# A fused attention and two-expert-layer kernel: one route's search by counting on TensorE, a zero-padded key chunk, and some squares on GpSimd

## The chip, the cores and the metric

One Trainium2 chip, one core. The time is device microseconds from the first to the last instruction of one execution and what lies around it; lower is better. The kernel before has a median of 1275.76 us over 3 runs.

## What is computed

Three layers in a row, all in float32. First linear attention over 8 batches, 8 heads, 576 tokens and a head width of 64, normalized per head; then a mixture of 8 experts to which the 4608 tokens are assigned greedily, each expert taking at most 576 tokens; then a dense layer that takes the maximum of three products.

```python
def _attn_ref(q, k, v, g_norm):
    kv = np.einsum('bhsd,bhse->bhde', k, v)
    out = np.einsum('bhsd,bhde->bhse', q, kv)
    rms = np.sqrt(np.mean(out * out, axis=-1, keepdims=True) + 1e-06)
    return (out / rms * g_norm)

# mixture of experts: logits = x @ w_gate, sorted over all (token, expert) pairs
    for idx in order:
        tok, e = (int(idx) // E, int(idx) % E)
        if assigned[tok] >= 0 or counts[e] >= cap:
            continue
        assigned[tok] = e
        counts[e] += 1
    for e in range(E):
        mask = assigned == e
        out[mask] = np.maximum(x[mask] @ w1[e], 0.0) @ w2[e]

# last layer
    h = np.maximum(np.maximum(x @ w1, x @ w2), x @ w3)
    return h @ w_out
```

## The kernel before, in words

**Attention (lines 85 to 497).** Batches go in pairs (`bp`, four of them); the two batches of a pair are 1152 tokens, nine chunks of 128, and chunk 4 holds the end of one batch and the start of the next. `load` puts keys, values and queries in SBUF on the SP queue, each in a first part (`a`, five chunks) and a second part (`b`, four). `kv` (line 179) multiplies keys with values on TensorE, chunk by chunk, into one PSUM tile per batch; of chunk 4 each batch takes its own 64 rows (line 189), so one of its five matmuls has 64 rows. Every float32 matmul is two instructions. `o_tile` (line 214) multiplies one chunk of queries with the result; ScalarE squares the output (line 230) and copies it to `y` (line 234), VectorE sums the squares per head (line 235). `norm_a` and `norm_b` make the norms and the gate logits `L` per three chunks, and `y_store` writes `y` to DRAM on SP. The next pair's second query part goes into the same buffer as this pair's, and its load stands in SP's order behind this pair's stores.

**Routes.** In phase `p` the kernel picks the next expert that fills up, and the 576 tokens it takes. For that it needs the threshold logit above which a column has more than its places. Route 0 (`top_search`) runs between the attention and the experts, with nothing beside it: seven rounds, each comparing every token's key with 15 to 63 thresholds (VectorE), counting per expert with 36 matmuls whose weights are the one-hot choice (8 columns), comparing the counts with the capacity, and broadcasting the verdict with one more matmul. The routes 1 to 6 run beside the experts, in pieces: `phase` is a generator, and `tick` (line 914) runs it to its next `yield`; a tick comes after every column group of 12 big matmuls (after 24 in the output layer, none). There `search` (line 504) makes 16 steps on transposed keys: per step two sign sums on ScalarE (line 512) and one comparison on VectorE (line 514), `ce` (line 518), one matmul (line 523), and four small VectorE operations (lines 527 to 534) that give the next three thresholds. With `slow` (route 1 only) a step lasts three ticks for the first eight, otherwise two.

**Experts.** In stage `p` (0 to 7) TensorE multiplies the gathered rows `X` with `w1` (8 column blocks), the result with `w2` (4), that with the three matrices of the last layer (`W3`, 6 blocks of three), and last with `w_out`. All products are split in a high and a low part, three matmuls each (`mm3`, lines 888 to 890). VectorE rounds `H` (line 979) and `X` (line 997), and in stage 0 also splits the expert weights (line 838), which GpSimd does later.

**Decoding, in stage 0 only.** The 24 weight tiles of the last layer come as 64-bit words. A background generator (`decoder`) works on one piece per tick from the fifth on: shift (line 372, VectorE), merge (line 379, VectorE), add (line 380, GpSimd), round (lines 386 and 388, ScalarE), residual (line 394, VectorE, the first four on GpSimd; line 397, GpSimd). Its tiles share the buffer `xg` with the rows that are gathered, so `gather` may run only when all 24 are `ready`.

**Order of the work.** The order of each engine is the order of the Python calls (a manual schedule). At the end of a route `tick` calls `gather` if all 24 tiles are ready; otherwise it is called after the stage's last tick (line 1025). Then GpSimd scales the five row tiles (line 868), and the output matmuls (lines 1044 to 1046) alternate with the transposes of the next expert's rows (line 877).

## Time and profile before

| what | value |
|---|---|
| median of 3 runs | 1275.76 us (1274.73 to 1277.25) |
| the profiled execution's own time | 1274.72 us |
| its span | 1272.9 us |
| TensorE matmuls busy | 1208.8 us, 95% of the span |
| VectorE busy | 646.0 us, 51% |
| ScalarE busy | 482.3 us, 38% |
| GpSimd busy | 398.2 us, 31% |
| mean granted TensorE clock | 0.976 of full speed |

A page of the profile names each group of instructions by its line, engine and operation, and by its tiles as output<-inputs. A bracket at the end of a row of the timeline is the time its engine stood idle just before, and what it waited for. The rows of waits name the waiting instruction, then what released it, with the total, the number of times and the longest. Matmuls are pipelined, so a row's duration is longer than its distance to the next one; where a price per matmul is needed, starts are compared. TensorE is busy nearly all the time from 400 us on; before that it has gaps.

### The profile page before, as it was taken

The page shows a single profiled execution, that of the slowest core. Times are in us where ns is not written, and L with a number is a line of the kernel's source. Part 1 is how long each engine was busy: PE and PEld are TensorE (multiplying, and loading weights), DVE is VectorE, ACT ScalarE, POOL GpSimd, SP SyncE. Part 2 cuts the span into 40 slices and gives each one's busy share as a digit, 9 for nine tenths or more (in the row PEclk, how much of TensorE's full clock was granted, in tenths as well). Part 3 has the DMA queues.
Part 4 walks back from the last instruction along what each step waited for, and adds up shares of the span by engine and source line. Part 5 has one row for each costly group of instructions (what it writes and reads, how often), then busy time and mean ns, then how long its engine had stood idle before and what let it go on. Part 6 is the DMA issues. An engine that isn't in the chain of part 4 may idle for free.

```text
span 1272.9 us, 23272 instructions
## 1 busy us (share of the span) xinstructions
PE 1208.8 (95%) x8878; PEld 1136.6 (89%) x8880; DVE 646.0 (51%) x2075; ACT 482.3 (38%) x1166; POOL 398.2 (31%) x483
## 2 busy tenths in 40 slices
PE   9996698778999999999999999999999999999996
PEld 7885398777999989998999899999999899989995
DVE  2656688873576346653666167725763421121110
ACT  3547254651453136413542155314631331133110
POOL 0000123544521354135412451245214451253121
PEclk9998798889999999999999999999999999999998
DMA  9999410343330223121311232113312252023101
GB/s 342 396 380 355 150 59 25 118 148 105 109 100 26 80 75 109 34 94 54 102 65 59 64 117 84 59 47 108 100 35 70 76 161 86 1 75 109 59 1 42
DMA packets 52033, 136.15 MB, mean 107 GB/s; under 512 B 5840, under 2 KB 10448, under 8 KB 50384
## 3 DMA queue, kind: packets, MB, share of 16 engines
q1 hardware_dynamic: 44672, 110.25, 25.8%
q0 software_dynamic: 6944, 24.38, 5.7%
q8 instruction: 70, 1.15, 0.4%
q14 instruction: 43, 0.35, 0.1%
q10 hardware_dynamic: 304, 0.02, 0.0%
HBM read 111.43 MB, written 23.20 MB: 106 GB/s over the span
## 4 chain that ended last, share of the span: by engine, by line
PE 77%; DVE 12%; ACT 5%; issue 2%; DMA 2%; POOL 1%; POOLq 0%; SPq 0%; ACTq 0%; DVEq 0%
PE mm L888 19%; PE mm L890 18%; PE mm L889 18%; PE mm L1044 4%; PE mm L1046 4%; PE mm L1045 4%; PE kv L189 4%; ACT W L512 3%; PE o L225 2%; DVE T L534 2%; PE tp L877 1%; DVE w L394 1%; DVE w L379 1%; DVE dv L372 1%; DMA vtb<-vx_dram 1%
## 5 line engine op out<-in xcount | busy, mean ns | idle before, releaser
L888 PE MATMUL mm<-X,w 128*128 128x288 f32 x1152 | 346.9, 301 | 0.0
L890 PE MATMUL mm<-X,w 128*128 128x288 f32 x1152 | 341.3, 296 | 0.0
L889 PE MATMUL mm<-X,w 128*128 128x288 f32 x1152 | 341.2, 296 | 0.0
L888 PEld LDWEIGHTS mm<-X,w 128*128 128x128 f32 x1152 | 218.7, 190 | 0.4
L889 PEld LDWEIGHTS mm<-X,w 128*128 128x128 f32 x1152 | 218.2, 189 | 0.0
L890 PEld LDWEIGHTS mm<-X,w 128*128 128x128 f32 x1152 | 218.0, 189 | 0.0
L838 POOL TENSOR_TENSOR ring<-raw,ring 128x512 fp32r<-128x512 f32 x112 | 144.2, 1289 | 206.8 <-ACT ring L829 195.8
L1021 POOL TENSOR_TENSOR H<-t,H 128x288 fp32r<-128x288 f32 x96 | 77.8, 810 | 417.1 <-ACT H L1020 417.0
L1019 DVE TENSOR_TENSOR t<-mm,t 128x288 f32<-128x288 f32 x192 | 87.1, 454 | 159.5 <-PE mm L890 157.8
L888 PE MATMUL mm<-H,ring 128*128 128x288 f32 x512 | 156.5, 306 | 0.0
L888 PE MATMUL mm<-X,ring 128*128 128x288 f32 (+1 forms) x512 | 153.7, 300 | 1.6 <-ACT X L883 1.6
L889 PE MATMUL mm<-H,ring 128*128 128x288 f32 x512 | 152.3, 297 | 0.0
L890 PE MATMUL mm<-H,ring 128*128 128x288 f32 x512 | 152.1, 297 | 0.0
L890 PE MATMUL mm<-X,ring 128*128 128x288 f32 (+1 forms) x512 | 151.1, 295 | 0.6 <-DVE X L884 0.6
L889 PE MATMUL mm<-X,ring 128*128 128x288 f32 (+1 forms) x512 | 150.7, 294 | 0.0
L512 ACT ACTIVATE W<-KT,T 96x384 bf16<-96x384 f32 x168 | 102.1, 608 | 117.3 <-DVE T L534 117.3
L1020 ACT CAST H<-t 128x288 fp32r<-128x288 f32 x96 | 41.4, 432 | 231.6 <-DVE t L1019 231.6
L888 PEld LDWEIGHTS mm<-X,ring 128*128 128x128 f32 x512 | 96.4, 188 | 2.2 <-ACT X L883 2.1
L888 PEld LDWEIGHTS mm<-H,ring 128*128 128x128 f32 x512 | 98.0, 191 | 0.0
L889 PEld LDWEIGHTS mm<-H,ring 128*128 128x128 f32 x512 | 97.5, 190 | 0.0
L890 PEld LDWEIGHTS mm<-H,ring 128*128 128x128 f32 x512 | 97.2, 190 | 0.0
L890 PEld LDWEIGHTS mm<-X,ring 128*128 128x128 f32 x512 | 96.1, 188 | 1.1 <-DVE X L884 1.1
(257 smaller groups left out, 2037.4 us busy)
## 6 DMA issues: line engine op xcount, KB each, us to landing
raw<-w_dram SPq DMA_DIRECT2D x128, 256.0 KB, 2.7
ring<-wod SPq DMA_DIRECT2D x48, 512.0 KB, 3.5
xd<-y SPq DMA_DIRECT2D x36, 288.0 KB, 9.4
w<-w_dram SPq DMA_DIRECT2D x18, 512.0 KB, 8.2
qta<-qx_dram SPq DMA_DIRECT2D x4, 1280.0 KB, 15.0
qtb<-qx_dram SPq DMA_DIRECT2D x4, 1024.0 KB, 12.4
kta<-kx_dram SPq DMA_DIRECT2D x3, 1280.0 KB, 17.6
vta<-vx_dram SPq DMA_DIRECT2D x3, 1280.0 KB, 16.6
```

The source lines that it names most:

```text
L189: nc.tensor.matmul(KV[b][:, hp, :], KT[bp, o][p0:p1, c - o * CA, h], VT[bp, o][p0:p1, c - o * CA, h], start=(i == 0), stop=(i == len(cs) - 1))
L512: nc.scalar.activation(gs[:, j], KT, AF.Sign, bias=T[0:96, 1 + j:2 + j], scale=-1.0, accum_out=cnt[:, j:j + 1])
L838: (nc.gpsimd if stream[m][0] else nc.vector).tensor_sub(t[:, 1], raw, t[:, 0])
L888: nc.tensor.matmul(ps, wt[:, 0, ws], x[:, 0, xs], start=first, stop=False)
L889: nc.tensor.matmul(ps, wt[:, 1, ws], x[:, 0, xs], start=False, stop=False)
L890: nc.tensor.matmul(ps, wt[:, 0, ws], x[:, 1, xs], start=False, stop=last)
L1019: nc.vector.tensor_tensor(t2, ps[:, :HS], (t1, t1, t2)[j], op=OP.max)
L1020: nc.scalar.copy(m[:, 0, cs], t2)
L1021: nc.gpsimd.tensor_sub(m[:, 1, cs], t2, m[:, 0, cs])
L1044: nc.tensor.matmul(pss[c], l[:, 0, ls], w[:, 0, :], start=(fc == 0), stop=False)
L1045: nc.tensor.matmul(pss[c], l[:, 0, ls], w[:, 1, :], start=False, stop=False)
L1046: nc.tensor.matmul(pss[c], l[:, 1, ls], w[:, 0, :], start=False, stop=(fc == 5))
```

## The change

1. *Key chunk 4.* The first part of the keys is loaded without it (four chunks). It goes into a tile of its own, `ZK`, twice: once with the lower 64 rows and zeros above, once the other way. The zeros are set once on GpSimd; the rows come in two small transfers per pair (on ScalarE's queue for the first pair, on SP's after that). All `kv` matmuls then have 128 rows.
2. *Squares.* For the middle chunk of each three (not among the last three of all) the square is computed on GpSimd from the copied `y`. Its reduction on VectorE is put off until the next chunk's.
3. *Route 1* (`p == 1`) no longer transposes its keys; `count_search` makes seven rounds in the manner of route 0, with the route's own limits per expert. A round lasts four ticks: two from the comparison to the 36 matmuls, two from these to the broadcast. Its tables `TH`, `SV` and `th0` move to a pool that lives on, the thresholds in bfloat16. The other routes go through `sign_search`, which is the old code moved.
4. *Gather.* `tick` calls `gather` in any tick from which on the route is done and all 24 tiles are ready, and from the seventh tick after that scales one row tile per tick; what is left is scaled at the end of the stage.

```diff
+    ZK = []
+    for i in range(2):
+        z = ld.tile([128, 2, DM], F32, name="zk%d" % i)
+        nc.gpsimd.memset(z[64:128, 0], 0.0)
+        nc.gpsimd.memset(z[0:64, 1], 0.0)
+        ZK.append(z)
...
-                nc.sync.dma_start(KT[bp, 0][:, :, h0:h1], kx[bp, :, 0:CA, h0:h1])
+                nc.sync.dma_start(KT[bp, 0][:, :, h0:h1], kx[bp, :, 0:CA - 1, h0:h1])
                 nc.sync.dma_start(VT[bp, 0][:, :, h0:h1], vx[bp, :, 0:CA, h0:h1])
+            for r in range(2):
+                p = slice(64 * r, 64 * r + 64)
+                (nc.sync if bp else nc.scalar).dma_start(ZK[bp % 2][p, r], kx[bp, p, CA - 1])
...
-            for i, (c, p0, p1) in enumerate(cs):
+            for i, c in enumerate(cs):
                 o = int(c >= CA)
-                nc.tensor.matmul(KV[b][:, hp, :], KT[bp, o][p0:p1, c - o * CA, h], VT[bp, o][p0:p1, c - o * CA, h],
+                kt = ZK[bp % 2][:, r, h] if c == CA - 1 else KT[bp, o][:, c - o * CA, h]
+                nc.tensor.matmul(KV[b][:, hp, :], kt, VT[bp, o][:, c - o * CA, h],
...
-        nc.scalar.activation(sq, pv[:, :, :, 0:128], AF.Square)
+        pool = gi == 1 and c < NT - 3
+        if not pool:
+            nc.scalar.activation(sq, pv[:, :, :, 0:128], AF.Square)
...
-        nc.vector.tensor_reduce(SS[0][:, gi], sq.rearrange("p a b (h d) -> p (a b h) d", d=D),
-                                axis=AX, op=OP.add)
+        if pool:
+            ys = Y[0][:, gi, :, 0:128].rearrange("p (a b) d -> p a b d", a=2)
+            nc.gpsimd.tensor_mul(sq, ys, ys)
+        RQ.append((SS[0][:, gi], sq))
+        while RQ and not pool:
+            ss, sq = RQ.pop(0)
+            nc.vector.tensor_reduce(ss, sq.rearrange("p a b (h d) -> p (a b h) d", d=D), axis=AX, op=OP.add)
...
+    def count_search(g2, K, L2, oh):
...
+        for i in range(7):
+            J = STEPS[i - 1][1] if i else J0
...
+                if ns is None:
+                    nc.vector.tensor_tensor(gs[-1], kc, th, op=OP.is_ge)
+                else:
+                    nc.vector.scalar_tensor_tensor(gs[-1], kc, ns, th, op0=OP.subtract, op1=OP.is_ge)
+                if not i:
+                    yield
+            if ns is not None:
+                nc.vector.tensor_scalar(K, K, ns, None, op0=OP.subtract)
+            yield
+            yield
+            pc = rps.tile([128, 512], F32, name="rps")
+            for c in range(NT):
+                nc.tensor.matmul(pc[0:E, 0:J], oh[:, :, c], gs[c // nt][:, c % nt, :], start=(c == 0),
+                                 stop=(c == NT - 1))
+            ex = rt.tile([E, 64], BF, name="ex8")
+            nc.vector.tensor_scalar(ex[:, 0:J], pc[0:E, 0:J], lim, None, op0=OP.is_gt)
+            yield
+            yield
+            pb = rps.tile([128, 512], F32, name="rps")
+            nc.tensor.matmul(pb[:, 0:J], ones8, ex[:, 0:J], start=True, stop=True)
...
+            nc.vector.scalar_tensor_tensor(sc[:, 0:J], pb[:, 0:J], 0.5, SV[:, i:i + 1].to_broadcast([128, J]),
+                                           op0=OP.is_ge, op1=OP.mult, accum_out=ns)
...
+            if p == 1:
+                for r in count_search(g2, sf, best, oh):
...
+            else:
+                flags = yield from sign_search(g2, V, sf, best, oh, REM2)
...
             except StopIteration:
                 route = None
-                if len(ready) == 24:
-                    gather(len(XG) // 5)
+        if route is None and 0 < len(IDX) < E + 1 and len(XG) < 5 * len(IDX) and len(ready) == 24:
+            fetch[:] = [[len(IDX) - 1, 0, list(range(5))]]
+            gather(len(IDX) - 1)
```

Three places show what the engines get in another order.

VectorE in stage 0, one search step of route 1 before: from the comparison that follows a new threshold (line 514, tile `W`) to the next threshold (line 534, `T`). `ce` feeds the search matmul; line 394 is a weight residual, line 372 a decode shift, line 379 a decode merge.

```order
L514 TENSOR_SCALAR W_2806,cnt<-KT,T_2803 96x384
L1019 TENSOR_TENSOR t_2720<-mm,t_2720 128x288
L379 SCALAR_TENSOR_TENSOR w_22_1224<-w_22_1224,dv 128x512
L518 TENSOR_TENSOR ce<-BM,cnt 96x24
L394 TENSOR_TENSOR w_11_2848<-dv,w_11_2848 128x512
L372 TENSOR_SCALAR dv<-w_23_1226 128x512
L527 TENSOR_TENSOR ex<-rps,REM_1925 128x24
L529 TENSOR_REDUCE an<-ex 128x3
L531 TENSOR_SCALAR ex,tot<-an 128x3
L534 TENSOR_SCALAR T_2863<-SC,T_2803,tot 128x4
```

The same engine now, one round in the W3 layer: verdict (line 654), comparison (635), shift of the keys (639); then, past other work (rounding of X, 1086; merges, 397; shifts, 390; maxima, 1108; residual, 412), the comparison of the counts (647).

```order
L654 SCALAR_TENSOR_TENSOR scr,ns<-rps,SV 128x15
L635 SCALAR_TENSOR_TENSOR W_2821<-K_2699,ns,TH 128x540
L639 TENSOR_SCALAR K_2699<-K_2699,ns 128x36
L1086 TENSOR_TENSOR X<-mm,X 128x288
L397 SCALAR_TENSOR_TENSOR w_20_1232<-w_20_1232,dv 128x512
L390 TENSOR_SCALAR dv<-w_11_1234 128x512
L647 TENSOR_SCALAR ex_2901<-rps,lim_2035 8x15
L1108 TENSOR_TENSOR t_2827<-mm,t_2826 128x288
L397 SCALAR_TENSOR_TENSOR w_11_1234<-w_11_1234,dv 128x512
L1108 TENSOR_TENSOR t_2827<-mm,t_2827 128x288
L412 TENSOR_TENSOR w_10_2938<-dv,w_10_2938 128x512
L390 TENSOR_SCALAR dv<-w_21_1236 128x512
```

The five small operations and `ce` of a step are gone from between the decode rows; a round has one comparison and three small operations, and two ticks' work of others stands between the comparison and the verdict on the counts.

SP, from the loads for the third pair to its predecessor's second query part (`qtb`); `DMAHW` numbers are the eight completion lanes, and an entry waits for the transfer that used its lane last. Before:

```order
L98 DMA kta<-kx_dram 128x2560
L99 DMA vta<-vx_dram 128x2560 [waits DMAHW3_49]
L271 DMA xd<-y 128x576 [waits DMAHW4_49,Pool_49]
L271 DMA xd<-y 128x576 [waits DMAHW5_49,Activation_49]
L271 DMA xd<-y 128x576 [waits DMAHW6_49,Activation_49]
L271 DMA xd<-y 128x576 [waits DMAHW7_49,Pool_49]
L271 DMA xd<-y 128x576 [waits DMAHW0_49,Activation_49]
L271 DMA xd<-y 128x576 [waits DMAHW1_49,Activation_49]
L107 DMA qtb<-qx_dram 128x4x512 [waits DMAHW2_49,PE_49]
```

Now:

```order
L104 DMA kta<-kx_dram 128x2048 [waits DMAHW6_49]
L105 DMA vta<-vx_dram 128x2560 [waits DMAHW7_49]
L108 DMA zk_132<-kx_dram 64x512 [waits DMAHW0_49]
L108 DMA zk_132<-kx_dram 64x512 [waits DMAHW1_49]
L289 DMA xd<-y 128x576 [waits DMAHW2_49,Activation_49,Pool_49]
L289 DMA xd<-y 128x576 [waits DMAHW3_49,Activation_49]
L289 DMA xd<-y 128x576 [waits DMAHW4_49,Activation_49]
L289 DMA xd<-y 128x576 [waits DMAHW5_49,Activation_49,Pool_49]
L289 DMA xd<-y 128x576 [waits DMAHW6_49,Activation_49]
L289 DMA xd<-y 128x576 [waits DMAHW7_49,Activation_49]
L116 DMA qtb<-qx_dram 128x4x512 [waits DMAHW0_49,PE_49]
```

The two `zk` transfers stand behind the values, and `qtb` waits for the lane of the first of them, where it waited for the lane of the keys (`kta`).

GpSimd at the end of stage 0: subtractions for H (line 1021, now 1110), the gather (862, now 945) and the scaling of the gathered rows (868, now 951). Before:

```order
L1021 TENSOR_TENSOR H<-t_3388,H 128x288
L1023 CAST LO<-H 128x2x64
L1021 TENSOR_TENSOR H<-t_3467,H 128x288
L1021 TENSOR_TENSOR H<-t_3515,H 128x288
L1023 CAST LO<-H 128x2x64
L862 DMA xg<-xd,idx 128x576 x5
L868 TENSOR_TENSOR xg<-xg 128x4x128 x5
L838 TENSOR_TENSOR ring<-raw,ring 128x512 x4
```

Now:

```order
L398 TENSOR_TENSOR dv<-w_17_3336 128x512
L1110 TENSOR_TENSOR H<-t_3359,H 128x288
L945 DMA xg<-xd,idx 128x576 x5
L1110 TENSOR_TENSOR H<-t_3420,H 128x288
L1112 CAST LO<-H 128x2x64
L1110 TENSOR_TENSOR H<-t_3489,H 128x288
L1110 TENSOR_TENSOR H<-t_3535,H 128x288
L1112 CAST LO<-H 128x2x64
L951 TENSOR_TENSOR xg<-xg 128x4x128 x3
L1110 TENSOR_TENSOR H<-t_3585,H 128x288
L951 TENSOR_TENSOR xg<-xg 128x4x128 x2
L1110 TENSOR_TENSOR H<-t_3634,H 128x288
L1112 CAST LO<-H 128x2x64
```

The gather moved ahead of the last five H subtractions, and the scalings between them.

## Rows read from the trace of the kernel before

**Rows 1.** Timeline of TensorE (start us, us, engine, line, what): where stages begin

```profile
157.56 0.39 PE L888 MATMUL mm<-X,ring 128*128 128x256 f32 x1 [0.78 <-ACT X L883]
...
164.44 0.29 PE L888 MATMUL mm<-X,ring 128*128 128x288 f32 x1
...
327.24 0.38 PE L888 MATMUL mm<-X,ring 128*128 128x288 f32 x1
...
464.89 0.38 PE L888 MATMUL mm<-X,ring 128*128 128x288 f32 x1
...
597.17 0.38 PE L888 MATMUL mm<-X,ring 128*128 128x288 f32 x1
```

**Rows 2.** Waits of TensorE, 150 to 335 us: total us, times, longest

```profile
PE rps L523 <- DVE ce L518: 18.7, 9, 5.5
PE tp L877 <- POOL xg L868: 4.0, 1, 4.0
```

**Rows 3.** Timeline of TensorE at two search steps of stage 0

```profile
185.76 0.19 PE L523 MATMUL rps<-ce,ones 96*128 96x24 bf16 x1
...
186.02 0.29 PE L889 MATMUL mm<-X,ring 128*128 128x288 f32 x1
186.15 0.29 PE L890 MATMUL mm<-X,ring 128*128 128x288 f32 x1
...
238.05 0.20 PE L523 MATMUL rps<-ce,ones 96*128 96x24 bf16 x1 [5.48 <-DVE ce L518]
```

**Rows 4.** Busy us by window: PE, PEld, DVE, ACT, POOL, clock, DMA share, GB/s

```profile
200.00:210.00 10.00, 7.32 (x39) 7.09 (x38) 8.43 (x25) 4.43 (x12) 2.08 (x2) 0.71 0.08 26
...
30.00:60.00 30.00, 27.64 (x214) 24.70 (x213) 17.39 (x53) 17.41 (x38) 0.82 (x4) 1.00 1.02 395
```

**Rows 5.** Timeline of TensorE in the attention

```profile
16.33 0.49 PE L189 MATMUL kv<-vta,kta 64*128 64x128 f32 x2
16.74 1.16 PE L189 MATMUL kv<-vtb,ktb 128*128 128x128 f32 x8
17.74 0.60 PE L200 MATMUL bt<-ident,BD 128*128 128x128 f32 x4
...
55.68 1.22 PE L225 MATMUL o<-BD,qtb 128*128 128x144 f32 x8 [0.79 <-DMA qtb<-qx_dram]
...
80.97 1.22 PE L225 MATMUL o<-BD,qtb 128*128 128x144 f32 x8 [0.33 <-DMA qtb<-qx_dram]
82.11 0.45 PE L341 MATMUL rps<-G,oh 128*8 128x63 bf16 x9
```

**Rows 6.** Waits, all engines, 0 to 150 us

```profile
PE o L225 <- ACT y L234: 2.0, 4, 1.3
```

**Rows 7.** Chain that ended last, in order of time: one burst of 36 small matmuls

```profile
422.96 1.00 PE rps L656 x36
```

**Rows 8.** VectorE's groups, 157 to 304 us (busy us, mean ns, idle before)

```profile
L379 DVE SCALAR_TENSOR_TENSOR w<-w,dv 128x512 int32<-128x512 int32 x24 | 20.3, 847 | 0.0
L394 DVE TENSOR_TENSOR w<-dv,w 128x512 fp32r<-128x512 f32 x14 | 14.1, 1004 | 9.2 <-ACT w L386 9.1
...
L372 DVE TENSOR_SCALAR dv<-w 128x512 int32<-128x512 int32 x19 | 10.3, 541 | 0.0
L838 DVE TENSOR_TENSOR ring<-raw,ring 128x512 fp32r<-128x512 f32 x13 | 9.5, 736 | 0.0
...
L979 DVE SCALAR_TENSOR_TENSOR H<-mm,H 128x288 fp32r<-128x288 f32 (+2 forms) x16 | 7.2, 454 | 2.6 <-ACT H L976 2.3
```

**Rows 9.** Timeline of VectorE in route 0: the comparison in three pieces

```profile
119.71 1.78 DVE L583 SCALAR_TENSOR_TENSOR W<-H,ns,TH 128x372 bf16<-128x372 f32 x3
```

**Rows 10.** GpSimd's groups, 155 to 330 us: scaling of the gathered rows

```profile
L868 POOL TENSOR_TENSOR xg<-xg 128x512 f32<-128x512 f32 x5 | 5.1, 1050 | 0.0
```

**Rows 11.** Waits of the SP queue, 0 to 150 us

```profile
SPq L107 <- DMA kta<-kx_dram: 5.4, 2, 2.7
```

More of the change, by code (lines that the diff above doesn't have):

```diff
@@ L502, in bc, with search @@
         return ap[:, :, None].to_broadcast([128, E, NT])
-    def search(KT, i0, i1, REM2, slow):
+    def search(KT, i0, i1, REM2):
         T = SC[:, i0]
@@ L677, in finish, with sign_search @@
         yield
+    def sign_search(g2, V, sf, best, oh, REM2):
+        KT = []
+        for i, key in enumerate((sf, best)):
+            K = V.rearrange("p e c -> p (e c)").rearrange("p (g e c) -> p g e c", g=3, e=E)
+            for g in range(3):
+                gs = slice(12 * g, 12 * g + 12)
+                nc.vector.tensor_mul(K[:, g], oh[:, :, gs], key[:, None, gs].to_broadcast([128, E, 12]))
+            yield
+            yield
+            pt = rps.tile([128, 512], F32, name="rps")
+            for g in range(3):
+                nc.tensor.transpose(pt[0:96, g * 128:g * 128 + 128], K[:, g].rearrange("p e c -> p (e c)"),
+                                    ident)
+            KT.append(rt.tile([128, 384], F32, name="KT", tag="KT" + str(i))[0:96])
+            nc.scalar.copy(KT[i], pt[0:96, 0:384])
+            yield
+        b1 = None
+        for r in search(KT[0], 0, 11, REM2):
+            if r is None:
+                yield
+            else:
+                b1 = r
+        H1 = rt.tile([128, 1], F32, name="H1")
+        nc.vector.tensor_scalar(H1, b1, 0.5, None, op0=OP.max)
+        nc.vector.scalar_tensor_tensor(KT[1], KT[0], H1[0:96], KT[1], op0=OP.is_equal, op1=OP.mult)
+        yield
+        nc.vector.tensor_scalar(KT[0], KT[0], H1[0:96], 3000.0, op0=OP.is_gt, op1=OP.mult)
+        nc.vector.tensor_add(KT[0], KT[0], KT[1])
+        t = rt.tile([128, NT], F32, name="kt")
+        nc.vector.scalar_tensor_tensor(t, sf, H1, best, op0=OP.is_equal, op1=OP.mult)
+        nc.vector.tensor_scalar(sf, sf, H1, 3000.0, op0=OP.is_gt, op1=OP.mult)
+        nc.vector.tensor_add(sf, sf, t)
+        yield
+        b2 = None
+        for r in search(KT[0], 11, 16, REM2):
+            if r is None:
+                yield
+            else:
+                b2 = r
+        L1 = rt.tile([128, 1], F32, name="L1")
+        nc.vector.tensor_scalar(L1, b2, 1.0, None, op0=OP.add)
+        return commit(g2, sf, L1, oh)
     def phase(p):
@@ L712, in phase @@
             yield
-            KT = []
-            for i, key in enumerate((sf, best)):
-                K = V.rearrange("p e c -> p (e c)").rearrange("p (g e c) -> p g e c", g=3, e=E)
-                for g in range(3):
-                    gs = slice(12 * g, 12 * g + 12)
-                    nc.vector.tensor_mul(K[:, g], oh[:, :, gs], key[:, None, gs].to_broadcast([128, E, 12]))
-                yield
-                yield
-                pt = rps.tile([128, 512], F32, name="rps")
-                for g in range(3):
-                    nc.tensor.transpose(pt[0:96, g * 128:g * 128 + 128], K[:, g].rearrange("p e c -> p (e c)"),
-                                        ident)
-                KT.append(rt.tile([128, 384], F32, name="KT", tag="KT" + str(i))[0:96])
-                nc.scalar.copy(KT[i], pt[0:96, 0:384])
-                yield
@@ L912, in body @@
     beat = 0
+    fetch = []
     def tick():
@@ L918, in tick @@
             bg_piece(1)
+        for f in fetch:
+            f[1] += 1
+            if f[1] > 6 and f[2]:
+                scale(f[0], f[2].pop(0))
         if route is not None:
@@ L1024, in body @@
         drain()
-        if (p + 1, 0) not in XG and p + 1 < E:
-            gather(p + 1)
         if p + 1 < E:
-            for c in range(5):
-                scale(p + 1, c)
+            if (p + 1, 0) not in XG:
+                gather(p + 1)
+                fetch[:] = [[p + 1, 0, list(range(5))]]
+            while fetch[0][2]:
+                scale(p + 1, fetch[0][2].pop(0))
         odd = p % 2
```

78 lines of the change are left out of this document (42 added, 36 removed).

## The prediction

> **What bounds the kernel now.** I read the starts of the stages first, then who waits for whom on TensorE, then single places on its timeline. A stage is one expert; it begins with the first big matmul of the first layer. Stage 0 begins at 157.56 us, stage 1 at 327.24, stage 2 at 464.89, stage 3 at 597.17 [rows 1]. Stage 2 does the work of stage 0 (four output tiles, one search beside it) in 132.28 us; stage 0 takes 169.68 us. These 37.4 us are what the search part of the change can reach. In the waits of TensorE over stage 0, 18.7 us in 9 waits stand at the matmul of a search step that needs `ce` from VectorE, and 4.0 us at the transposes of the next expert's rows, which wait for GpSimd [rows 2]; the longest single wait is 5.48 us [rows 3]. The waits also cost clock: between 200 and 210 us TensorE was busy 7.32 of 10 us and the granted clock was 0.71 of full, a mix of its levels 1.2 and 2.4 GHz [rows 4]. So the excess is 18.7 + 4.0 booked, some 4 at the start (below), and the rest, about 11 us, lower clock and short gaps.
>
> The attention ahead of it has two limits that lie close together. TensorE stops at the second part of the queries of two batch pairs until it has landed, 0.79 us at 55.68 and 0.33 us at 80.97, while the DMA engines are booked full (share 1.02, 395 GB/s from 30 to 60 us) [rows 4, 5]. ScalarE holds TensorE up for 2.0 us in 4 waits [rows 6].
>
> **The change part by part.** All sums are against the profiled execution, 1274.7 us (span 1272.9); the median of the runs shown is 1.0 above it.
>
> *Search of the second route.* Sixteen steps of counting by signs become seven rounds of 36 small matmuls and one broadcast matmul. Added on TensorE: the first round has 63 columns, and nine such matmuls show 0.45 us [rows 5], so 36 cost 1.8; the other six have 31 or 15 columns, and a burst of 36 with 36 columns takes 1.00 us in the chain [rows 7], so 6.0. A lone small matmul between big ones: from the search matmul at 185.76 to the second big one after it at 186.02 are 0.26 us where big ones follow each other in 0.13 [rows 3], so it costs 0.13; seven broadcasts cost 0.9. Together 8.7 us. Removed: 16 search matmuls at 0.13, 2.1 us (six transposes go too; not counted).
>
> The waits. A step today passes three queues (VectorE sets the threshold, ScalarE makes two sign sums, VectorE makes `ce`) within 36 or 24 big matmuls. A round passes VectorE twice (compare; then the verdict), and 24 big matmuls, 24 x 0.13 = 3.1 us, stand before each of its two stops on TensorE: 14 stops. Whether VectorE keeps up is a count of its rows. A round lasts 48 x 0.13 + 1.1 = 7.4 us on TensorE. In the w2 layer VectorE has in it two decode merges (0.847 each), two residual subtractions of decoded weights (1.004), two decode shifts (0.541), two splits of expert weights (0.736) and two roundings of X (0.45, as those of H) [rows 8], 7.2 us, and of the search the compare and four small operations. The compare of 540 elements is three of today's 180-element ones; I take it by the 372-element one, 1.78 us for three [rows 9], so 0.9 at most, and the rest as 0.7: 8.8 us, 1.4 too much, in four rounds 5.6. In the w1 layer four roundings (0.454 each) stand for two, there is one shift and no subtraction, and the compare has 1116 elements (1.8): 8.1 against 7.4, in two or three rounds 1.0 to 2.1. In the W3 layer no split is left and it fits. That gives some 6 to 7 us of waits; the means contain the stretches that GpSimd's and ScalarE's load causes today, and ScalarE loses all sign sums, so I take 6. The ends: 0, if these stretches go; 18.7, today's sum [rows 2].
>
> *Earlier gather.* The route now ends after 600 of the stage's 816 big matmuls, where it ended after 804. The gather then waits only for the last decoded weight, and stands on GpSimd ahead of the last five H subtractions instead of behind all twelve; three of five scalings (1.05 us each [rows 10]) follow ahead of the last but one, two ahead of the last. The 4.0 us wait at the transposes goes. What is late next there: nothing, since the output matmuls of two weight chunks still lie between. In stages 1 to 6 only the scalings move, on an engine nobody waits for there: 0.
>
> *Stage 0 anew:* 132.3 (stage 2) - 2.1 + 8.7 + 3.8 (start: from 157.56 to 164.44 are 6.9 us for 24 big matmuls worth 3.1, because the transposes of the last rows lie between [rows 1]) + 6 = **148.7**, against 169.7: **-21.0**.
>
> *Zero-padded key chunk.* Two matmuls over 64 rows take from 16.33 to 16.74, 0.205 each; eight over 128 rows from 16.74 to 17.74, 0.125 each [rows 5]. There are 64 of the first kind, 16 per batch pair: 16 x 0.08 = 1.3 us per pair, 5.1 in all. The Trainium skill speaks against it: "TensorE: Matmul & The Clock Gate", the section "Why this matters for your kernels", has a matmul over few rows take as long as one over all 128, so that padding would bring nothing; by it the sum would be 1.3 us higher. The row says 0.08 us each, and I go by the row.
> But the first three pairs end in a wait for queries that the full DMA queue sets [rows 5]; what TensorE saves before it, it waits there. I count the last pair only, 1.3. The four zero fills on GpSimd (64x512) and the two loads on ScalarE's queue at the start lie under the warm-up matmuls; if the first loads slip, the same gate takes it up.
> On SP two small transfers per pair come between. The load of the queries waits today for the landing of the eighth transfer before it, 2.7 us each time [rows 11]; that transfer was a first part of keys and is now a small one that lands behind the values. So it is issued about 3 us later; while six stores are queued ahead of it that costs nothing, otherwise up to 3 us in each of two pairs. I take 0.
>
> *Squares on GpSimd.* Eleven of 36 go from ScalarE; gain at most the 2.0 us of rows 6, and before the gate nothing. Each reduction then waits for the next tile; for tile 31, on the way to the last logits, a square (1.05 us by rows 10) against ScalarE's own puts its reduction behind one more norm. I take +0.5. Attention: **-0.8** (from -7 to +6).
>
> **Sum:** 1274.7 - 21.0 - 0.8 = 1252.9; as a median 1.0 more: **1254**.
>
> **Rivals.**
> *VectorE still sets the pace (0.15).* For: it has no slack in stage 0 by the count above. Against: it loses the sign count and five small operations per step. The waits stay 18.7: 1254 + 12.7 = 1267.
> *The stops wait longer than the steps did (0.06), the other side.* Each of 14 stops halts all big matmuls behind it, and a late compare of 1116 elements halts 36 matmuls. It decides from (21.0 + 0.8 + 6) / 14 = 2.0 us per stop; the worst today is 5.48, the mean 18.7 / 16 = 1.2. At 3 us: 1254 - 6 + 42 = 1290.
> *Queries land later (0.10):* 3 us in each of two pairs: 1260.
> *The DMA gate gives way (0.12):* keys and stores are issued earlier by a faster TensorE, and the whole 5.1 and 2.0 arrive: 1254 - 5.8 = 1248. Against: share 1.02.
> *The padding gains nothing (0.07):* the 0.08 us belongs to the switch between row counts and not to the 64 rows: 1255. By the skill's rule above this is what comes.
>
> **How the numbers follow.** The forecast has 0.50. The range leaves out the slower rival and the far part of VectorE's pace, and takes in waits from 0 (1248) together with part of the gate: 1246 to 1264. A measurement of this kernel tells about 0.2%, 2.6 us, from no change. Slower 0.07 (the second rival and a little of the third), same 0.03 (the upper end of the first), faster 0.90.
>
> **What would show it.** Right: stage 0 lasts 146 to 152 us and stages 1 to 6 as before; TensorE's waits in it are for the compare or the verdict and stay under 8 us together; the clock has no slice under 0.9 between 190 and 280; the wait of 4.0 us for the scaled rows is gone; 64-row key matmuls are gone and the wait for the queries is longer by 1 to 3 us in two pairs. Wrong: waits at the count matmuls of over 1.2 us each, a compare that takes over 2 us, a gather that still ends the stage, or stage 1 beginning later than 165 us after the start of stage 0.

## The result: 11.9 us of the 21.8 forecast

The changed kernel takes 1263.91 us, the median of 3 runs (1263.52 to 1265.83), against 1275.76: a ratio of 0.991 (0.9887 to 0.9932). The forecast was 1254, with a range of 1246 to 1264, at whose far end the result lies. Run again later it came to 0.988 (0.9857 to 0.9903). Its profiled execution took 1263.5 us, with a span of 1261.8.

The starts of the stages on TensorE's timeline of the changed kernel (start, duration, instruction) show where the gain sits and where it stops.

```profile
157.75 0.58 PE L971 MATMUL mm<-X,ring 128*128 128x256 f32 x1 [0.78 <-ACT X L966]
...
166.26 0.30 PE L971 MATMUL mm<-X,ring 128*128 128x288 f32 x1
...
315.73 0.38 PE L971 MATMUL mm<-X,ring 128*128 128x288 f32 x1
...
453.50 0.38 PE L971 MATMUL mm<-X,ring 128*128 128x288 f32 x1
```

Stage 0 lasts 158.0 us; it was 169.7 [rows 1] and was forecast at 148.7. It begins as late as before (157.75 against 157.56), and from stage 1's start to the end of the span are 946.1 us against 945.7. So the whole gain is 11.7 us in stage 0. The sum forecast 1252.9 for the profiled execution, which took 10.6 more: 9.3 of them lie in stage 0, 1.0 ahead of it (it begins 0.2 later where 0.8 earlier was forecast), the rest behind it.

TensorE's waits from 150 to 335 us (waiting instruction, releaser, total, times, longest) are the counterpart of [rows 2]:

```profile
PE mm L960 <- DVE xg L951: 3.2, 2, 2.9
PE rps L682 <- DVE tots L674: 2.7, 1, 2.7
PE rps L723 <- DVE W L717: 2.0, 2, 1.0
PE rps L845 <- DVE c L839: 1.6, 1, 1.6
...
PE rps L644 <- DVE W L633: 0.7, 1, 0.7
PE rps L644 <- DVE W L635: 0.6, 2, 0.3
PE rps L737 <- DVE R L729: 0.3, 1, 0.3
```

The 18.7 us of the search and the 4.0 us of the transposes are gone. The 14 stops of the count search (L644 and L651) wait 1.3 us together. What waits now is the part of the route that follows the search, its finish: the count of what was chosen (`c`, L845), the totals (`tots`, L682), the positions (`W`, L723), their sum (`R`, L737), 6.6 us. (The 3.2 us for `xg` lie ahead of the stage.) In the kernel before, the finish came when the decode was over; now it lies in the middle of it. The windows show the clock around these waits (busy time of TensorE, its weight loads, VectorE, ScalarE, GpSimd; granted clock; DMA share; GB/s):

```profile
230.00:240.00 10.00, 9.28 (x69) 8.96 (x69) 7.68 (x14) 4.13 (x8) 7.40 (x8) 1.00 0.29 109
240.00:250.00 10.00, 6.38 (x45) 6.15 (x45) 8.97 (x27) 3.26 (x8) 4.09 (x5) 0.90 0.29 105
250.00:260.00 10.00, 10.00 (x61) 10.00 (x61) 9.86 (x18) 5.44 (x10) 8.56 (x9) 0.76 0.46 143
260.00:270.00 10.00, 7.66 (x77) 6.95 (x76) 8.62 (x18) 4.24 (x8) 5.55 (x7) 0.83 0.40 133
```

Behind the gaps the clock is 0.76 and 0.83 of full, a mix of 1.2 and 2.4 GHz. On the timeline of stage 0, from the first big matmul of 288 columns on, 48 big matmuls follow each other at about 0.24 us instead of 0.13: 5.0 us, where stage 2 has 23 and 2.0.

That clock is one of this execution. In another execution of the same kernel (the run "the same again" below; that first matmul starts at 169.41, so its times are 3.15 us later) the gaps for `c` and `tots` are the same, and the clock behind them stays at 1.00:

```profile
240.00:250.00 10.00, 7.48 (x56) 7.10 (x54) 9.07 (x22) 2.41 (x5) 5.83 (x7) 1.00 0.41 151
250.00:260.00 10.00, 8.17 (x63) 8.16 (x64) 9.76 (x22) 4.51 (x10) 6.59 (x7) 1.00 0.18 58
260.00:270.00 10.00, 5.38 (x59) 4.99 (x58) 8.62 (x14) 5.49 (x11) 7.54 (x8) 0.72 0.60 205
```

There only 26 big matmuls are slow (2.7 us), and still nothing is gained: TensorE comes to the matmuls for `W` earlier and waits longer. The row for the first of them in either execution, the second with the clock held:

```profile
262.35 0.62 PE L723 MATMUL rps<-W,W 128*32 128x36 bf16 x18 [1.01 <-DVE W L717]
...
265.49 0.72 PE L723 MATMUL rps<-W,W 128*32 128x36 bf16 x18 [3.71 <-DVE W L717]
```

Both begin 96.1 us behind the first matmul of 288 columns. So up to `W` it is VectorE that sets the time, and the slow matmuls ahead of it only fill a wait.

VectorE's timeline in the same place shows two reasons why the finish is late:

```profile
246.56 1.09 DVE L857 SCALAR_TENSOR_TENSOR A<-M,dx,gt 128x36 f32<-128x36 f32 x1
...
252.72 2.81 DVE L390 TENSOR_SCALAR dv<-w 128x512 int32<-128x512 int32 x1
...
260.45 1.84 DVE L717 TENSOR_TENSOR W<-hb,iot 128x576 bf16<-128x576 bf16 x1
...
265.61 0.69 DVE L412 TENSOR_TENSOR w<-dv,w 128x512 fp32r<-128x512 f32 x1 [1.31 <-ACT w L404]
```

Operations that last 0.25, 0.42 and 0.75 us elsewhere take 1.09, 2.81 and 1.84 while GpSimd works on the decode; and the queue stands still in front of a decode subtraction (L412) until ScalarE has made its cast: 11.0 us in 8 waits from 200 to 280 us. The route's small operations stand behind both.

### The profile page after: what moved, and what is told of

It is laid out like the page before. It is cut to its first block, busy times and chain, and to the rows that moved or that the text cites. A ratio compares the mean times of both kernels' runs of the same rounds, so it can differ in the third digit from the quotient of the medians.

```text
span 1261.8 us, 23567 instructions
## 1 busy us (share of the span) xinstructions
PE 1206.0 (96%) x9117; PEld 1140.8 (90%) x9117; DVE 635.4 (50%) x1974; ACT 457.3 (36%) x1089; POOL 415.2 (33%) x498
## 3 DMA queue, kind: packets, MB, share of 16 engines
q8 instruction: 71, 1.16, 0.4%
## 4 chain that ended last, share of the span: by engine, by line
PE 76%; DVE 12%; DMA 6%; ACT 3%; issue 2%; SPq 1%; POOL 0%; POOLq 0%; ACTq 0%; DVEq 0%
PE mm L971 20%; PE mm L973 19%; PE mm L972 19%; PE mm L1134 4%; PE mm L1136 4%; PE mm L1135 4%; DMA zk<-kx_dram 3%; ACT W L530 2%; DVE T L550 1%; DMA vta<-vx_dram 1%; PE tp L960 1%; DVE dv L390 1%; PE o L234 1%; PE kv L198 1%; DMA xd<-y 1%
## 5 line engine op out<-in xcount | busy, mean ns | idle before, releaser
L530 ACT ACTIVATE W<-KT,T 96x384 bf16<-96x384 f32 x140 | 85.1, 608 | 87.3 <-DVE T L550 87.3
L971 PEld LDWEIGHTS mm<-X,ring 128*128 128x128 f32 x512 | 96.9, 189 | 2.3 <-ACT X L966 2.1
L973 PEld LDWEIGHTS mm<-X,ring 128*128 128x128 f32 x512 | 96.6, 189 | 0.8 <-DVE X L967 0.8
L971 PEld LDWEIGHTS mm<-H,ring 128*128 128x128 f32 x512 | 96.7, 189 | 0.2
L972 PEld LDWEIGHTS mm<-X,ring 128*128 128x128 f32 x512 | 96.8, 189 | 0.0
L972 PEld LDWEIGHTS mm<-H,ring 128*128 128x128 f32 x512 | 96.4, 188 | 0.0
```

What stands on the lines that cost most here:

```text
L530: nc.scalar.activation(gs[:, j], KT, AF.Sign, bias=T[0:96, 1 + j:2 + j], scale=-1.0, accum_out=cnt[:, j:j + 1])
L971: nc.tensor.matmul(ps, wt[:, 0, ws], x[:, 0, xs], start=first, stop=False)
L972: nc.tensor.matmul(ps, wt[:, 1, ws], x[:, 0, xs], start=False, stop=False)
L973: nc.tensor.matmul(ps, wt[:, 0, ws], x[:, 1, xs], start=False, stop=last)
```

## The experiments

Each changes the changed kernel unless it says otherwise. A ratio is to the kernel before, timed beside it on the same chip; stage 0 is read off the starts like the 158.0 above. At first there were two theories: A, the finish lies in the decode with too few turns between its steps (a turn is one `tick`); B, VectorE is short of time in stage 0 whatever the order.

| run | stage 0, us | of it behind the start | waits of TensorE in the finish, us | ratio (95%) |
|---|---|---|---|---|
| changed kernel | 158.0 | 149.5 | c 1.6, tots 2.7, W 2.0, R 0.3 | 0.991 (0.9887 to 0.9932) |
| the same again | 157.8 | 149.5 | c 1.6, tots 2.7, W 4.6 | 0.988 (0.9857 to 0.9903) |
| more turns | 159.9 | 151.9 | tots 1.6, W 3.9, R 3.0 | 0.9899 (0.9882 to 0.9915) |
| finish held back | 155.9 | 147.4 | c 7.3 | 0.9872 (0.9855 to 0.9888) |
| fillers in the waits | 156.1 | 149.2 | W 3.6 | 0.9892 (0.9875 to 0.9908) |
| lag | 154.0 | 145.5 | tots 2.5, W 2.5, R 0.2 | 0.9847 (0.983 to 0.9863) |
| subtractions on VectorE | 155.8 | 147.7 | tots 2.7, W 2.4 | 0.987 (0.9853 to 0.9886) |
| lag, subtractions on VectorE | 153.2 | 145.0 | tots 1.6, W 2.9 | 0.986 (0.9843 to 0.9876) |
| lag, 1 + 1 turns | 153.7 | 146.9 | tots 0.9, W 2.8, R 2.5 | 0.9876 (0.9859 to 0.9892) |
| lag, 2 + 2 turns | 161.6 | 153.2 | R 9.5 | 0.9911 (0.9883 to 0.9938) |
| the same, subtractions on VectorE | 155.1 | 147.0 | W 1.1, R 5.8 | 0.9862 (0.9838 to 0.9886) |
| lag, late tiles held | 156.3 | 148.1 | tots 3.3 | 0.9889 (0.9872 to 0.9905) |
| lag, 1 + 1 turns, late tiles held | 157.2 | 148.7 | tots 1.8 | 0.99 (0.9883 to 0.9916) |
| old gather | 164.6 | 156.1 | c 1.6, tots 2.7, W 3.2 | 0.9929 (0.9911 to 0.9948) |
| old attention | 158.3 | 149.8 | c 1.6, tots 2.7, W 3.2 | 0.9894 (0.9877 to 0.991) |
| key chunk on GpSimd's queue | 156.0 | 149.2 | c 1.6, tots 2.7, W 3.2 | 0.9877 (0.9853 to 0.9901) |
| warm start | 157.6 | 149.3 | c 1.6, tots 2.7, W 4.6 | 0.9875 (0.9852 to 0.9897) |
| best | 151.4 | 143.1 | tots 0.3, W 1.6, R 1.0 | 0.9819 (0.98 to 0.9838) |
| kernel before | 169.7 | 162.8 | c 0.7; search 18.7, transposes 4.0 | 1 |
| kernel before, lag | 163.6 | 156.7 | search 14.4, transposes 4.0 | 0.9934 (0.991 to 0.9958) |

The start (to the first big matmul of 288 columns, 157.75 to 166.26 above) took 6.9 to 8.5 us with the same instructions; behind it, five executions whose kernels do not differ in the stage agree within 0.6 us (149.2 to 149.8). So the third column is what I compare, one execution each. The waits vary more: W's is 2.0 to 4.6 us in these five, with the clock behind `tots`. What they agree in is where the matmuls for `W` begin: 96.0 to 96.1 us behind the start in all five. The ratios, with some 0.2% to either side, order the runs less sharply.

**More turns, or later, or filled.** In `phase` and `finish`, for route 1, `for _ in range(n): yield` ahead of the matmul for `c` (n = 1), for `tots` and for `W` (2 each); the one for `tots`:

```
         nc.vector.tensor_scalar(tots[:, 1:2], ...
         yield
         yield
+        for _ in range(2 if p == 1 else 0):
+            yield
```

> The changed kernel, with more turns of the big matmul loop (each turn is one step of the route) between VectorE's work and the small matmuls that read it, in the part of the second route behind the count search: one more ahead of the c2 count, two more ahead of the totals (tots), two more ahead of the position matmuls (W). Theory A (the finish of the route, which now falls where the decode's VectorE work runs, leaves TensorE waiting 1.6 us for the counts, 2.7 us for tots and 2.0 us for W, and the clock falls from these gaps): the three waits go under 1.5 us together, the granted clock in 240 to 270 us stays at 0.9 or more in each 10 us, stage 0 lasts 148 to 152 us instead of 158.0, the time is 1253 to 1257. Rival B (VectorE's work in stage 0 is the bound, so a wait that is taken away comes back at the next stop or at the transposes of stage 1): waits of stage 0 keep their sum within 2 us, the time stays at 1261 to 1265.

Held back: `for _ in range(14): yield` behind `count_search`.

> The changed kernel, with the finish of the second route held back by 14 turns of the big matmul loop right after the count search, so that it falls where the decode has ended; the slack between its steps is that of the changed kernel. Theory A (the waits come from the finish running beside the decode's VectorE work): the waits for the counts, tots and W go to under 2 us together as in the kernel before; the gather is later and may cost 0 to 4 us at the transposes of stage 1; the time is 1253 to 1259. Rival B (VectorE's total work bounds stage 0): no gain, 1261 to 1266.

Filled: `heat(7, ...)`, `heat(12, ...)`, `heat(5, ...)` at the three places.

> The changed kernel, with filler matmuls (128x128 by 512, bfloat16) on TensorE while it waits at the three places of the finish: 7 ahead of the c2 count, 12 ahead of the tots matmuls, 5 ahead of the W matmuls. The waits stay, the engine is not idle in them. If some 5 us of the loss is the clock that falls after these gaps (theory A's second half), the granted clock between 240 and 270 us stays at 0.9 or more and the time is 1257 to 1260. Rival: the clock falls for another reason, or the fill costs what it saves: 1262 to 1266.

More turns made it worse: the stage is 2.4 us longer behind its start, `W` begins at 100.6 instead of 96.1, and the waits (8.5 us; 6.6 and 8.9 in the changed kernel's two executions) have only moved further down the finish, as B has it. Held back, the finish met one wait of 7.3 us at its first step, and gained 2.0 us. So A in this form falls. The fillers kept the clock at 1.00 until 260 us (0.83 from there), but of the 1.9 us that stage 0 is shorter 1.6 lie in its start: `W` begins at 96.1 as it did without them. The execution whose clock stayed at 1.00 without fillers says the same. A filler alone does not help while VectorE is the one that is late.

**VectorE's stops.** The decode's last step, one piece later:

```
-        for n in range(ND + 3):
-            if n >= 3:
-                dec_d(ORDER[n - 3])
+        for n in range(ND + 4):
+            if n >= 4:
+                dec_d(ORDER[n - 4])
```

> The changed kernel with the decode's last step (the low half, subtracted on VectorE behind ScalarE's cast) issued one decode piece later. Theory C (VectorE falls behind in stage 0 because its queue stands still for 13.5 us between 200 and 280 us, each time behind a decode subtraction that waits for ScalarE's cast; the route's steps queue behind it): VectorE's waits for the cast go under 5 us, TensorE's waits in the finish (now 1.6, 2.7 and 2.0 us) fall by half or more, stage 0 lasts 152 to 155 us, ratio 0.986 to 0.989. Rival B (VectorE has no more room, whatever the order): TensorE's waits keep their sum within 2 us, ratio 0.990 to 0.993.

The 11.0 us in front of L412 (13.5 in the expectation) are gone from VectorE's waits from 200 to 280 us; what is left is another line:

```profile
DVE dv L390 <- ACT w L385: 4.8, 2, 3.0
```

Stage 0 lost 4.0 us, the wait for `c` is gone and `W` begins at 92.7, but tots and W still wait 2.5 each. Theory C is right that the stops make the backlog, and not that they make all of it. The same edit in the kernel before:

> The kernel before, with the decode's last step one piece later and nothing else. VectorE waited 9.0 us for the cast between 200 and 280 us there too. If VectorE's stops cost the kernel before as much as they cost the changed one, stage 0 falls from 169.7 to 164 to 167 us and the ratio is 0.995 to 0.998; if they only bite once the search's finish comes to lie among the decode, stage 0 stays within 1.5 us of 169.7 and the ratio is 0.999 to 1.002.

There it took 6.1 us from stage 0 (search waits 18.7 to 14.4). The stops are nothing that the change brought in: they cost the kernel before more than the changed one.

**GpSimd beside VectorE.** In `dec_d`, tiles 18 to 23:

```
-            nc.gpsimd.tensor_sub(w[:, 512:1024].bitcast(F32R), ...
+            nc.vector.tensor_sub(w[:, 512:1024].bitcast(F32R), ...
```

> The changed kernel with the low half of the decode's tiles 18 to 23 subtracted on VectorE instead of GpSimd (6 subtractions: 1.47 us each on GpSimd, 0.69 us each on VectorE when it is alone). Theory E (what puts VectorE behind is that its operations last longer beside GpSimd's: 2.81 us for an operation of 0.42, 1.84 for one of 0.75): the long forms go from the finish, VectorE's own sum between 235 and 265 us falls in spite of the added 4.1 us, TensorE's waits in the finish fall by 2 us or more, ratio 0.987 to 0.990. Rival: VectorE has 4 us more to do and is later by that: waits of the finish grow by 2 to 4 us, ratio 0.992 to 0.996.

Six more subtractions on VectorE made stage 0 shorter, by 1.7 us behind its start. From 200 to 280 us the merges (L397) take 682 ns each instead of 829 and the shifts (L390) 673 instead of 719, and the waits for the cast fall from 11.0 us to 6.8, with 1.9 more in front of the moved subtractions. `W` begins at 93.6. Of the finish's waits only that for `c` is gone; TensorE is simply there earlier. Together with the lag:

> The lag, with the low half of tiles 18 to 23 on VectorE, no extra turns. Alone the lag took 3.9 us from stage 0 and the moved subtractions 2.2 us. If the two are separate causes (VectorE's stops, and the stretching beside GpSimd), stage 0 lasts 151 to 153 us and the ratio is 0.981 to 0.985; if both only relieve the same backlog, 153.5 to 155 us, ratio 0.985 to 0.988.

That is 0.5 us less than with the lag alone (145.0 against 145.5), no more than the scatter, and not 1.7: both relieve mostly the same backlog.

**Lag and turns.**

> The changed kernel with the decode's last step one piece later (as in e6_lag) and two more turns ahead of the totals and of the position matmuls (two of e1_slack's three places). Alone, the lag left waits of 2.5 us for tots and 2.5 us for W; alone, the slack moved its waits on behind a VectorE that stood still. If both are needed (theory F: VectorE's stops behind the cast make the backlog, and the finish has one or two turns too few on top of it), the two waits go under 1.5 us together, stage 0 lasts 149 to 152 us instead of 154.0, ratio 0.981 to 0.984. Rival: the backlog comes back in R or at stage 1's transposes, as with the slack alone: stage 0 154 to 157 us, ratio 0.984 to 0.988.

> As e9_lag_slack, with the low half of the tiles 18 to 23 on VectorE as well (as in e8_sub_dve, which took 2.2 us from stage 0). If stretching beside GpSimd still counts once the stops are gone, stage 0 is 1 to 2 us shorter than in e9_lag_slack; if VectorE has slack by then, or is now short of room by the added 4.1 us, the same within 1 us or longer.

The edits of the lag and of the turns (2 and 2, none for `c`), without and with the moved subtractions. Both miss their numbers (the second by being 6.2 us shorter than the first behind the start, where I had said 1 to 2), and the first is the most telling run of the study: c, tots and W no longer wait, and R waits 9.5 us. VectorE's timeline of that kernel, and ScalarE's row that released it:

```profile
266.74 0.68 DVE L412 TENSOR_TENSOR w<-dv,w 128x512 fp32r<-128x512 f32 x1
272.13 0.43 DVE L390 TENSOR_SCALAR dv<-w 128x512 int32<-128x512 int32 x1 [4.72 <-ACT w L385]
273.31 0.46 DVE L1114 TENSOR_TENSOR t<-mm,t 128x288 f32<-128x288 f32 x1 [0.75 <-ACT t L1111]
273.68 0.72 DVE L397 SCALAR_TENSOR_TENSOR w<-w,dv 128x512 int32<-128x512 int32 x1
274.32 0.17 DVE L732 CAST R<-rps 32x32 bf16<-32x32 f32 x1
```
```profile
271.45 0.65 ACT L385 ACTIVATE w<-w 128x512 f32<-128x512 f32 x1 [6.23 <-DMA w<-w_dram]
```

R is an operation of 0.17 us. It stood behind the first decode step of tile 17, which waits for ScalarE's scaling, which waits for the tile's packed words. Those come late by their chain: tiles 12 to 17 use the buffers of 18 to 23, and each load waits until such a tile has been decoded and written out (in the changed kernel SyncE stands 60.6 us in front of these loads, in 6 waits, for the write-outs). So the finish runs between two walls: before some 260 us VectorE is full (9.86 of 10 us above), and from there its queue stands still for loads. The 7.3 us of the run that was held back are the second wall too: there ScalarE waited 6.26 and 3.08 us for packed words. In the changed kernel the finish just gets past. That the loads' chain is what makes the second wall is read from these waits; a kernel with tiles 18 to 22 decoded up to two places earlier, which would have tested it, gave no result. Theory G puts the two walls together:

> The changed kernel with the lag of e6_lag and one more turn (not two) ahead of the totals and of the position matmuls. Theory G (two deadlines close in on the finish: too few turns between its steps before some 262 us, and from there VectorE's queue stands still behind decode pieces whose packed weights have not landed, so that whatever part of the finish is still to come, waits there): tots and W wait under 2 us together, R waits some part of the 9.5 us that it waited with two turns each, 2 to 6 us; stage 0 lasts 153 to 158 us (154.0 with the lag alone, 161.6 with two turns each). If slack simply costs what it adds, stage 0 is half way, 157 to 158.5, with the waits where they were.

> As e21_lag_slack1, and the decode pieces of tiles 12 to 17 (those whose weights land last) are issued only once the second route is done, then two a turn. Theory G: nothing on VectorE's queue is left for R to wait behind: R's wait goes under 1 us, and stage 0 lasts 149 to 153 us, unless the third group of matmuls now waits for tile 14 (0 to 3 us more, to be seen as a wait of the big matmuls for w3). If the wait for R is not from these pieces, it stays as in e21_lag_slack1.

> The lag and the hold of tiles 12 to 17, without extra turns. By theory G the finish of e6_lag is past before the pieces that stand still (R waited 0.2 us there), so the hold takes only VectorE's work of those pieces out of the finish: waits of 2.5 us (tots) stay, W's 2.5 us fall to under 1.5 us, stage 0 152.5 to 154.5 us against 154.0.

The hold, in `decoder` at tile 12, with two pieces a turn once the route is done (short):

```
+            while n == 18 and route is not None and not force:
+                ...
+                yield
```

One turn each gave what G gives for tots (0.9) and R (2.5); W's 2.8 stayed, now at ScalarE's half of it (L715), which came behind a scaling (L385) that had waited 4.82 us for packed words. So none, one and two turns on top of the lag are 145.5, 146.9 and 153.2 us: more room, more time. With the late tiles held, R's wait is gone, as G has it. But the stage did not gain: TensorE now waited for the held tiles themselves, more than the 0 to 3 us I allowed, at a clock of 0.66 from 270 to 280 us:

```profile
PE mm L990 <- ACT w L404: 3.7, 1, 3.7
...
PE mm L991 <- DVE w L412: 2.3, 1, 2.3
```

and without extra turns 3.2 us at the same place. The decode's tail is as tight as the route.

**The other parts.**

> The changed kernel with the old rule for the gather of stage 1 (fetched when the route's last step is done, scaled in one go at the stage's end). Theory A (the gather's move is worth what the wait at the transposes was, 4.0 us, and a little clock behind it): the wait of about 4 us for xg at stage 1's transposes comes back and the time is 1266 to 1270. Rival: the route ends earlier now, so the old rule also fetches in time, and nothing is lost: 1262 to 1265, no wait for xg.

Edit: the changed kernel's rule in `tick` and its early scalings taken out. The wait of 4.0 us for `xg` came back and stage 0 was 6.6 us longer. From the last matmul ahead of that wait to the end of the stage are 5.8 us more than in the changed kernel: the wait and the lower clock behind it (0.89 in 300 to 310 us). The rest lies ahead of it and is not assigned.

> The changed kernel with the attention of the kernel before (no zero-padded key chunk, all squares on ScalarE); the search and the gather stay new. My forecast's attention term was -0.8 us, and the trace of the changed kernel has the first count burst 0.7 us earlier: so this kernel should have that burst at 118.2 us again and a time within 1.5 us of the changed kernel's ratio to the kernel before (0.990 to 0.993). Rival: the attention's edits are worth 2 us or more (ratio 0.993 or above) or cost something (ratio under 0.9895).

Edit: `kv`, `load` and `o_tile` taken from the kernel before. The ratio is that of the changed kernel. The first count burst came at 117.8 us; with the new attention it came between 117.1 and 120.4 in the runs here, so 0.7 us cannot be seen. In that run no wait of TensorE for the queries shows; in the changed kernel it is 6.1 us.

> The changed kernel with the small transfers of the shared key chunk (second to fourth pair) issued from GpSimd's queue instead of SyncE's, so that SyncE reaches the queries' transfer (qtb) sooner. If the queries land later in the changed kernel because SyncE issues them later (my forecast took that as nothing: the transfers are bound by bandwidth), the waits for qtb fall from 6.1 to 4 us or less and the first count burst comes at 116 to 117 us instead of 117.5; the ratio 0.988 to 0.991. If bandwidth sets it: waits within 0.7 us of 6.1, burst at 117.5 to 118.5, ratio 0.990 to 0.993.

```
-                (nc.sync if bp else nc.scalar).dma_start(ZK[bp % 2][p, r], kx[bp, p, CA - 1])
+                (nc.gpsimd if bp else nc.scalar).dma_start(ZK[bp % 2][p, r], kx[bp, p, CA - 1])
```

The waits for qtb fell to 3.4 us, but the products with it began at 57.37 us (56.40 in the changed kernel) and 82.25, and the burst came at 117.7. SyncE issued the first of these loads 3.5 us earlier (44.11 instead of 47.64) and it landed no earlier, so SyncE's later issue is not what holds it.

> The changed kernel once more, beside the next two on the same chip. Its ratio to the kernel before was 0.991 with an interval from 0.9887 to 0.9932; the experiments on one or two stages put it at 0.989 to 0.992. Stage 0 within 1 us of 158.0.

> The changed kernel with 27 filler matmuls instead of 18 behind the first route's last step, so that TensorE is not idle in the wait for the first gathered rows (2.9 us ahead of stage 0's first transposes). My forecast gave the start of stage 0 3.8 us over its 3.1 us of work; in the changed kernel it took 5.4 (157.75 to 166.26 us), with the clock at 0.79 and 0.87 in 150 to 170 us; in some of the runs since it took 3.8. If the gap ahead of the transposes is what lowers the clock there, the start takes 2 to 3.5 us over its work, the clock in 160 to 170 us is 0.95 or more, and the time 1 to 3 us under e25_after_again. If not, no change, or up to 1 us more where the fillers run past the wait.

Edit: `heat(27, hp)` for `heat(18, hp)`. Wrong: the gap ahead of the transposes was filled, the start still took 8.3 us and the clock in 160 to 170 us was 0.84. All runs with a start of 6.9 have a clock of 1.00 in 160 to 170 us, the others 0.72 to 0.98; what decides between the two is open.

**The best version.** Lag, subtractions on VectorE, fillers for tots (5) and W (6), the warm start, and the key chunk on GpSimd's queue:

> Together: the decode's last step one piece later, the low half of tiles 18 to 23 on VectorE, fillers in the waits for tots (5) and W (6), 27 fillers at the start of stage 0, and the shared key chunk's transfers from GpSimd's queue. e18_lag_dve had stage 0 at 153.2 us, with 46 matmuls at half clock (4.7 us) and 1.6 and 2.9 us of waits. With the clock held, stage 0 lasts 149 to 152 us and the ratio is 0.981 to 0.985; if the fillers only cost what they take, 153 to 155 us and 0.986.

```profile
250.00:260.00 10.00, 8.37 (x86) 7.24 (x86) 9.93 (x20) 4.60 (x9) 6.77 (x8) 1.00 0.44 160
260.00:270.00 10.00, 9.04 (x71) 8.81 (x70) 6.45 (x19) 3.69 (x8) 2.23 (x4) 1.00 0.74 276
```

1256.07 us against 1278.54 for the kernel before and 1264.17 for the changed one on that chip: it beats both. The clock stays at 1.00 through the finish; against lag and subtractions alone (0.88 and 0.78 in these two windows) stage 0 is 1.8 us shorter, 1.0 of it between R's matmuls and the end of the stage, where no wait for VectorE follows that a slow matmul could fill. So here the fillers pay. This is one execution of each kernel, and no run tells from which lateness of VectorE on they do.

## Why the prediction missed, step by step

*What bounds it; the place.* Right: all of the gain is in stage 0.

*Added matmuls, 8.7 us.* Nearly right. A burst and its verdict, in the changed kernel:

```profile
203.74 1.06 PE L644 MATMUL rps<-W,oh 128*8 128x15 bf16 x36 [0.30 <-DVE W L635]
204.73 0.41 PE L971 MATMUL mm<-H,ring 128*128 128x288 f32 x1
...
208.13 0.18 PE L651 MATMUL rps<-ex,ones 8*128 8x15 bf16 x1
208.24 0.40 PE L971 MATMUL mm<-H,ring 128*128 128x288 f32 x1
```

The first burst added 1.33 us over the big matmuls, the later ones 1.08 to 1.16, each verdict 0.2: 9.5 in all, 0.8 more than forecast.

*The waits at the 14 stops, "so I take 6".* This is the step that failed, in place and in size. I counted VectorE's rows round by round for the search and stopped where the search stops. The stops waited 1.3 us. The finish, which the change moves from the end of the stage into the decode, I took at its old price of nearly nothing; it waits 6.6. Together 7.9 for 6. The sum also has no term for the clock behind the waits, which the first paragraph had read off the kernel before: net of stage 2's own 2.0 us it is 3.0. The two are not separate terms, though: in the other execution the waits are 10.2 us (8.9 of them in the finish) and the clock is 0.7, and the stage lasts the same. The sentence "What is late next there: nothing" was said of the gather and is right for it; for the route itself it was never asked.

*The start, 3.8.* It took 5.4 in this execution (8.5 us for the same 24 matmuls), 1.6 more; three other runs had 3.8. With 0.8, 1.9, 3.0 and 1.6, 7.3 of the 9.3 us are placed; 2.0 I cannot assign. (The other execution gives 0.8, 4.2, 0.7 and 1.4, and leaves the same 2.0.)

*Earlier gather.* Right: the 4.0 us wait is gone, and undoing it costs 6.6 us of stage 0, more than the wait, in part because of the clock.

*Attention, -0.8.* The first burst came 0.7 us earlier, but runs scatter by more, so it is neither shown nor refuted. The mechanism behind it held: the padded matmuls are cheap, and the gate of the queries ate the gain. TensorE's timeline:

```profile
9.08 1.05 PE L198 MATMUL kv<-vta,kta 128*128 128x128 f32 x8
9.97 0.39 PE L198 MATMUL kv<-vta,zk 128*128 128x128 f32 x2
10.20 0.61 PE L198 MATMUL kv<-vta,kta 128*128 128x128 f32 x4
...
56.40 1.81 PE L234 MATMUL o<-BD,qtb 128*128 128x144 f32 x8 [4.47 <-DMA qtb<-qx_dram]
...
82.11 1.22 PE L234 MATMUL o<-BD,qtb 128*128 128x144 f32 x8 [1.62 <-DMA qtb<-qx_dram]
```

The padded pair takes 0.23 us, 0.115 each, where 64 rows took 0.205 [rows 5]. The Trainium skill, "TensorE: Matmul & The Clock Gate", section "Why this matters for your kernels", would have them equal; the two traces do not agree with it for these float32 matmuls (whether the 64 rows or the change of the row count cost it, no run separates). The waits for the queries, 0.79 and 0.33 us before, are 4.47 and 1.62, longer by 3.7 and 1.3 where I had said 1 to 3; the products behind them begin 0.7 and 1.1 us later than before, so the gate itself moved a little, which I had taken as nothing. The load of the first of them was issued 5.1 us later (47.64 against 42.56), where I had said about 3.

*The rivals.* "VectorE still sets the pace" is nearest: its time, 1267, came from waits that stay at the search; the mechanism, VectorE without slack in stage 0, is the one that the runs show, at another step. The slower rival did not come. One sign of being wrong did: a compare of 1116 elements took 2.19 us (the other one 1.38), but it held its stop up by 0.34 us only.

## What to carry to other kernels

When a chain of steps gets shorter, ask for every step behind it what it will run beside at its new time, and count the queue of the engine it shares there; the end of a chain that was free because its neighbours had finished is not free earlier. A step of 0.2 us on an in-order queue is as late as the load that the instruction ahead of it waits for, so extra distance between the steps can make it later, not earlier: find the instruction in front (here a decode step one piece too early) and move that. Half-speed matmuls behind a wait cost time only where no later wait takes it up: look at what the next stop waits for before you price or fill them.

## What the chip showed that I had not expected

From 240 to 250 us of the changed kernel TensorE was busy 6.38 us, and the granted clock was 0.76 over the next 10 us, in which it was busy throughout. In another execution of the same kernel, with the same gaps, it was 1.00 (250 to 260 us), as it was with the waits filled. In both the matmuls for `W` began 96.1 us behind the start. Filling the gap ahead of stage 0's start did not hold the clock (0.84 from 160 to 170 us).

Moving work from GpSimd to VectorE made a merge on VectorE 147 ns shorter and the stage 1.7 us, although VectorE was the engine that was late. (With the lag the stage gained 0.5 us by it.)

With the 64-row matmuls gone, the 128-row ones follow each other at 0.111 us (8 from 9.08 to 9.97), where they took 0.125 between 64-row ones before [rows 5].
